# Key products of five tile pairs as seven half products, with the folded query weights parked in device memory

## The chip, the cores and the metric

The kernel runs on one core of one Trainium2 chip. The core's engines are TensorE (PE for its matmuls, PEld for its weight loads), VectorE (DVE), ScalarE (ACT), GpSimd (POOL) and SyncE (SP, which here only issues DMAs). The metric is the time of one execution on the device in microseconds, the median over several runs; lower is better.

## The reference, cut to what matters

Input x is 2048 x 576, with 32 heads of 18. All data is float32.

```python
xn = layernorm(x)                                     # no affine part
q, k, v = split_heads(xn @ wqkv)
phi(t) = concat(softmax(t @ w_phi), softmax(-(t @ w_phi)))   # per head, 36 features
kv  = sum over rows of phi(k)^T v                     # per head 36 x 18
z   = sum over rows of phi(k)
o   = (phi(q) @ kv) / (phi(q) @ z + 1e-6)
s   = o @ wo
g   = silu((silu(xn @ w_gate) * (xn @ w_up)) @ w_down)   # 576 -> 4608 -> 576
return x + s * g
```

## The kernel before, in words

Every float32 operand is held as a high part and a low part, both float32r (`split`: the high part is a cast on ACT, the low part a subtraction on DVE). A product is then the sum of high x high, high x low and low x high, each a matmul of its own. Since 576 is 4.5 blocks of 128 rows, a 576-deep product is 14 matmuls: `xw` issues them, with the last half blocks folded into rows of one plane. `XB` holds the normalized x, transposed, in eight blocks of 512 columns: X00 to X13 in the listings.

The time goes through these stages.

1. Preparation (0 to 66.6 us): layer norm, transposes into `XB`, and `fold`, which multiplies the key and the query weights with w_phi once, so that phi needs one product per tile. The folded key weights and the value weights lie in `KVWH` (high parts, 3 planes of rows) and `KVWL` (low parts, 2 planes), the folded query weights in `QH` and `QL`.
2. Key/value stage (66.6 to 221.6 us): 16 tiles of 128 rows of x in eight pairs p. For each tile: the key product (`k_tile`, 28 matmuls of 288 columns into a bank pair `p2`), the two softmaxes (`softmax_parts`: on DVE max and min over a head and a subtraction for each, exp on ACT, sum on DVE; then reciprocal and multiply), the value product, and `kv_step`, which adds phi^T v into the banks `kvp`. In pairs 0 and 1 the value products are plain. From pair 2 on, the value products of the two tiles of a pair are computed together as seven half products (Strassen's scheme, `v_product`): the needed sums of the value weights are `TH` and `TL` (made by `v_sums` during pair 0, on POOL and ACT), the needed sums of x are `shi` and `slo` (made one pair ahead by `raw_x`, `sums` and `sum_parts`, on POOL and ACT, from `sraw`, one plane of which is loaded from `x_dram`).
3. Query stage (221.6 to about 460 us): 16 query tiles (`q_tile`), two at a time: product with `QH`/`QL` into `p2`, softmaxes as above into `e`, the denominator and the scaling of `e` on DVE (its last step is `last_e`, L626). Then, for each two tiles, transposes and the numerator (`numer`) and the product with wo (`project`).
4. FFN (to the end): gate and up products (L781) and down products (L898).

Between them lie "early tiles": products of the first FFN blocks f = 0 to 3 with `XB` (bank `pe`, L96, 28 matmuls of 512 columns for a tile of gate and up), whose results go to device memory. `early_weights` splits their weights (`raw` into `wh`, `wl`), `early_tile` does the products, Silu on ACT and a multiply with the up product on DVE (`h`, L135).

The order on each engine is fixed at build: a list scheduler places the instructions by its own costs, and `tc.high_priority()` and `tc.issue_after(instruction)` steer it. The holds that matter here refer to two lists: `read` collects the subtractions that read a bank pair (L316, two per `softmax_parts`), `exps` the last exp of each tile. These lines use them:

```python
parts = first_weights.pop() if f == 1 else early_weights(
    f, *{0: read[2 * NT + 1:2 * NT + 2], 2: (read[2 * NT + 3], exps[NT + 1])}.get(f, ()))
for i in halves:
    early_tile(f, i, parts, (1,) if f == 1 else (0, 1), behind=read[2 * NT + 1] if f == 1 else None)
```

NT is 16. `behind` holds the multiply of f = 1; for f = 0 and f = 2 the held instructions are those that split the weights. DMAs are issued in order on SP's queue unless another engine's is named.

## Time and profile before

| | before |
|---|---|
| median of 3 runs | 1594.09 us (1593.2 to 1594.78) |
| profiled execution, its time | 1594.86 us |
| its span on the core | 1592.7 us |
| PE busy | 1580.9 us, 99% |
| DVE busy | 1173.7 us, 74% |
| ACT busy | 724.5 us, 45% |
| POOL busy | 666.0 us, 42% |
| mean granted TensorE clock | 0.999 of full |

A row of the page's parts or of a view has a line of the kernel (L96), an engine, an operation, "out<-in" by the program's names without numbers (`p2` shows as `p`), shapes and counts. In the timeline the first number is the start in us from the beginning of the span, the second the duration, and a bracket at the end gives the idle time before and what released the engine. Matmuls overlap, so the distance between two starts, not the duration, is what one costs.

### The profile page before, as it was taken

Reading aid. Unit: us, or ns where it says so; the run is one execution under the profiler, and the core shown is the slowest. Engines: PE = TensorE matmul, PEld = TensorE weight load, DVE = VectorE, ACT = ScalarE, POOL = GpSimd, SP = SyncE. Lnnn points to the kernel's source line nnn. Section 1 sums busy time; section 2 is a strip of 40 time slices with the busy share of each in tenths; the row PEclk is TensorE's granted clock in tenths of the full one; section 3 lists DMA queues with packets and bytes.
Section 4 is the critical chain, followed back from the end, with each engine's and each line's share of the span. In section 5 each row is a group of like instructions: output and inputs, shape, how many; then the busy total and the mean of one; then the engine's idle time right before and its main releaser. Section 6 shows DMA issues by size and latency. Waiting matters only on the chain.

```text
span 1592.7 us, 25339 instructions
## 1 busy us (share of the span) xinstructions
PE 1580.9 (99%) x9383; PEld 1415.4 (89%) x9383; DVE 1173.7 (74%) x1729; ACT 724.5 (45%) x1403; POOL 666.0 (42%) x714
## 2 busy tenths in 40 slices
PE   9999999999999999999999999999999999999998
PEld 6899998999988988988888888888888888888887
DVE  7777769999946778987777878645667767666577
ACT  5633345455435654444454454454343333333334
POOL 2676762434126545554645535223324324133133
PEclk9999999999999999999999999999999999999999
DMA  9522244445456555555455453964545555565535
GB/s 306 199 82 80 95 148 127 118 124 164 160 181 239 177 180 177 177 173 181 171 183 190 154 188 116 346 212 149 154 142 156 184 180 159 180 183 178 145 117 179
DMA packets 124045, 269.04 MB, mean 169 GB/s; under 512 B 13194, under 2 KB 54858, under 8 KB 122642
## 3 DMA queue, kind: packets, MB, share of 16 engines
q1 hardware_dynamic: 108476, 245.49, 47.0%
q0 software_dynamic: 3552, 12.59, 2.7%
q10 hardware_dynamic: 11894, 9.35, 1.8%
q8 instruction: 74, 1.21, 0.3%
q14 instruction: 49, 0.40, 0.1%
HBM read 167.53 MB, written 99.09 MB: 167 GB/s over the span
## 4 chain that ended last, share of the span: by engine, by line
PE 69%; DVE 1%; POOL 0%; DMA 0%; issue 0%
PE px L781 25%; PE pd L898 24%; PE pw L781 12%; PE py L781 6%; POOL acc L936 0%; PE pe L96 0%; PE pd L781 0%; DMA out<-acc 0%; DVE hh L63 0%; DVE X L927 0%; DVE s L815 0%; DVE ha L831 0%; DVE acc L1098 0%; DVE acc L933 0%; DVE w L63 0%
## 5 line engine op out<-in xcount | busy, mean ns | idle before, releaser
L898 PEld LDWEIGHTS pd<-dw,hh 128*128 128x128 f32 x3012 | 423.8, 188 | 22.1 <-ACT pd L953 1.5
L898 PE MATMUL pd<-dw,hh 128*128 128x288 f32 x3012 | 438.3, 295 | 1.1 <-ACT pd L953 0.7
L781 PE MATMUL px<-X,w 128*128 128x512 f32 x1512 | 386.4, 390 | 0.0
L781 PEld LDWEIGHTS px<-X,w 128*128 128x128 f32 x1512 | 274.5, 188 | 48.9 <-ACT s L810 2.3
L781 PE MATMUL pw<-X,w 128*128 128x512 f32 x744 | 190.4, 391 | 0.0
L781 PEld LDWEIGHTS pw<-X,w 128*128 128x128 f32 x744 | 138.6, 188 | 29.1
L815 DVE TENSOR_TENSOR s<-pw,s 128x512 f32<-128x512 f32 x126 | 86.4, 687 | 97.7 <-ACT s L810 87.7
L1060 DVE TENSOR_TENSOR acc<-pd,acc 128x576 f32<-128x576 f32 x128 | 96.2, 752 | 77.7 <-PE pd L898 77.2
L810 ACT COPY s<-px 128x512 f32<-128x512 f32 x126 | 73.8, 586 | 156.3 <-PE px L781 156.3
L63 DVE TENSOR_TENSOR hh<-ha,hh 128x512 fp32r<-128x512 f32 x140 | 109.4, 807 | 22.2 <-ACT hh L62 21.4
L62 ACT CAST hh<-ha 128x512 fp32r<-128x512 f32 x140 | 82.7, 620 | 87.5 <-PE pd L898 74.2
L1032 POOL TENSOR_TENSOR hb<-hb 128x512 f32<-128x512 f32 x34 | 46.6, 1369 | 160.2 <-DVE hb L827 159.6
L96 PE MATMUL pe<-X,wh 128*128 128x512 f32 x340 | 105.7, 396 | 1.2 <-DVE h L135 0.7
L63 DVE TENSOR_TENSOR w<-ld,w 128x512 fp32r<-128x512 f32 (+1 forms) x96 | 80.5, 840 | 32.5 <-ACT w L62 31.0
L781 PE MATMUL px<-X,wt 128*128 128x512 f32 x252 | 98.0, 389 | 0.0
L1019 POOL TENSOR_TENSOR h<-ha,hb 128x512 f32<-128x512 f32 x34 | 44.4, 1307 | 126.4 <-DVE ha L831 93.9
L781 PE MATMUL py<-X,w 128*128 128x512 f32 x378 | 97.0, 391 | 0.0
L62 ACT CAST w<-ld 128x512 fp32r<-128x512 f32 (+1 forms) x96 | 52.7, 550 | 90.7 <-POOL ld L769 58.3
L1045 POOL TENSOR_TENSOR ha<-ha 128x512 f32<-128x512 f32 x34 | 52.6, 1564 | 94.9 <-DVE hh L63 94.9
L835 ACT COPY py<-px 128x512 f32<-128x512 f32 x63 | 36.0, 572 | 104.4 <-PE px L781 80.0
L766 POOL TENSOR_TENSOR ts<-ld 128x256 f32<-128x256 f32 x32 | 27.4, 855 | 129.9 <-issue 71.5
L781 PEld LDWEIGHTS py<-X,w 128*128 128x128 f32 x378 | 67.8, 188 | 10.6
(293 smaller groups left out, 3229.1 us busy)
## 6 DMA issues: line engine op xcount, KB each, us to landing
w_dram<-w SPq DMA_DIRECT2D x90, 512.0 KB
w<-w_dram SPq DMA_DIRECT2D x90, 512.0 KB
wt<-t_dram SPq DMA_DIRECT2D x62, 336.0 KB
ld<-in_B_w_gu SPq DMA_DIRECT2D x32, 512.0 KB
rt<-in_B_w_down SPq DMA_DIRECT2D x33, 288.0 KB
rb<-in_B_w_down SPq DMA_DIRECT2D x33, 288.0 KB
w_dram<-w SPq DMA_DIRECT2D x30, 256.0 KB
w<-w_dram SPq DMA_DIRECT2D x30, 256.0 KB
```

The costliest lines, as they stand in the source:

```text
L62: nc.scalar.copy(hi, src)
L63: nc.vector.tensor_sub(lo, src, hi)
L96: last = nc.tensor.matmul(ps, l, r, start=n == 0, stop=n == len(pairs) - 1)
L781: nc.tensor.matmul(ps, l, r, start=first and n == 0, stop=last and n == len(mm) - 1, skip_group_check=True)
L810: snaps.append(nc.scalar.copy(t, ps))
L815: nc.vector.tensor_add(t, ps, t)
L835: copies.append(nc.scalar.copy(yp, xp))
L898: nc.tensor.matmul(ps, l, r, start=first and n == 0 and m == 0, stop=n == len(hs) - 1 and m == 2, skip_group_check=True)
L1019: sub(s, g["h"][0][0], g["h"][0][1])
L1032: nc.gpsimd.tensor_add(a21, a21, g["h"][1][1])
L1045: sub(a12, a12, g["h"][0][0])
L1060: nc.vector.tensor_add(a2, pd[:, :, 0:HALF], a2)
```

## The change

For pairs 3 to 7 (`KS = 3`) the key products of the two tiles of a pair are computed as seven half products too, by a new function `pair`, which takes the place of the two `k_tile` calls; the x sums `shi` and `slo` that the value products use serve for the keys as well. The key weights' sums are new. They are made by `k_sums` in pair 1, on DVE, POOL and ACT, plane by plane (c = 0, 1, 2), in two column blocks of 160 and 128 (`wh` and `wl` from the early tiles' pool), with small DMAs on SP for the third plane's rows.

The sums lie where `QH` and `QL` were (tiles of the same names, called `KTH` and `KTL` in the code). So the folded query weights, 2.95 MB, are stored in `q_dram` after the fold and loaded again (`q_weights`, on SP) after the last key product of pair 7. Since the two tiles' key products end in SBUF rows and not in a bank pair, `softmax_rows` does their softmaxes; it appends to `exps`, and not to `read`. The kv steps of a pair and its last value product are carried over into the next pair (`steps`). All else is as before.

```diff
+KS = 3
+    q_dram = dram.tile([P, 2, 5, D], F32, name="q_dram")
...
+            def q_weights():
+                qs = [const.tile([P, 2, n, D], F32R, name=name) for n, name in ((3, "QH"), (2, "QL"))]
+                for t, c in zip(qs, (slice(0, 3), slice(3, 5))):
+                    nc.sync.dma_start(t.bitcast(F32), q_dram[:, :, c])
+                return qs
+
+            def softmax_rows(e):
+                m = kk.tile([P, 2, H], F32, name="m", bufs=1)
+                for s, op in enumerate((ALU.max, ALU.min)):
+                    nc.vector.tensor_reduce(m[:, s], heads(e[:, 0:D]), axis=AX.X, op=op)
+                for s in (1, 0):
+                    nc.vector.tensor_sub(heads(e[:, s * D:(s + 1) * D]), heads(e[:, 0:D]), spread(m[:, s], H))
+                    last = nc.scalar.activation(e[:, s * D:(s + 1) * D], e[:, s * D:(s + 1) * D], AF.Exp,
+                                                scale=1.0 if s == 0 else -1.0)
+                exps.append(last)
...
+            def k_sums():
+                spaces = [(epool.tile([P, 2, 2, 160], F32, name="wh", bufs=3), slice(0, 160)),
+                          (epool.tile([P, 2, 2, 128], F32, name="wl", bufs=3), slice(160, HALF))]
+                kh, kl = k_split(KVWH), k_split(KVWL)
+                nc.vector.memset(KTH[96:128, :, 2].bitcast(F32), 0.0)
+                for c in range(3):
+                    for r, n in spaces:
+                        rows = slice(0, P if c < 2 else 96)
+                        for k in range(2):
+                            if c == 2:
+                                for a in (0, 32):
+                                    nc.sync.dma_start(r[a:a + 32, k], kh[64:96, k, 2, :, n].bitcast(F32))
+                                nc.sync.dma_start(r[64:96, k], kh[0:32, k, 2, :, n].bitcast(F32))
+                            nc.vector.tensor_add(r[rows, k], kh[rows, k, c, :, n], kl[:, k, c, :, n] if c < 2 else r[rows, k])
+                        q = r[rows]
+                        nc.gpsimd.tensor_sub(q[:, 1, 0], q[:, 1, 0], q[:, 0, 0])
+                        nc.gpsimd.tensor_sub(q[:, 0, 0], q[:, 0, 0], q[:, 0, 1])
+                        nc.gpsimd.tensor_add(q[:, 0, 1], q[:, 0, 1], q[:, 1, 0])
+                        nc.gpsimd.tensor_sub(q[:, 1, 1], q[:, 1, 1], q[:, 0, 1])
+                        q = q.rearrange("p k m n -> p (k m) n")
+                        nc.scalar.copy(KTH[rows, :, c, n], q)
+                        if c < 2:
+                            nc.vector.tensor_sub(KTL[:, :, c, n], q, KTH[:, :, c, n])
+                        else:
+                            nc.vector.tensor_sub(KTH[64:96, :, 2, n], q[64:96], KTH[64:96, :, 2, n])
...
+            for n, (t, c) in enumerate(((QH, slice(0, 3)), (QL, slice(3, 5)))):
+                nc.sync.dma_start(q_dram[:, :, c], t.bitcast(F32))
+            KTH = const.tile([P, 4, 3, HALF], F32R, name="QH")
+            KTL = const.tile([P, 4, 2, HALF], F32R, name="QL")
...
+            def pair(n, x, kv0, v3, kv1):
+                v0, v1 = vbuf
+                phi0, phi1 = (kk.tile([P, 2 * D], F32, name="phi", bufs=2) for _ in range(2))
+                pk = kps.tile([P, 2, 512], F32, name="p2")
+                kx, ky = pk[:, 0], pk[:, 1]
+                k_product(kx, x[0], 0, True, False)
+                with tc.high_priority():
+                    nc.scalar.copy(ky[:, 0:HALF], kx[:, 0:HALF])
+                kv0()
+                v3()
+                k_product(ky, x[1], 2, False, True)
+                nc.scalar.copy(phi0[:, K1], ky[:, 0:HALF])
+                kw = kps.tile([P, 512], F32, name="vw")
+                kb = kk.tile([P, HALF], F32, name="kb", bufs=1)
+                k_product(kw, x[7], 1, True, False)
+                with tc.high_priority():
+                    nc.scalar.copy(kb, kw[:, 0:HALF])
+                k_product(kx, x[4], 4, False, False)
+                with tc.high_priority():
+                    nc.scalar.copy(phi0[:, K2], kx[:, 0:HALF])
+                k_product(kw, x[5], 3, False, True)
+                with tc.high_priority():
+                    nc.vector.tensor_add(phi0[:, K2], kw[:, 0:HALF], phi0[:, K2])
+                kv1()
+                k_product(kx, x[6], 5, False, False)
+                with tc.high_priority():
+                    nc.vector.tensor_add(phi1[:, K2], kx[:, 0:HALF], kb)
+                softmax_rows(phi0)
...
+                k_product(kx, x[3], 6, False, True)
+                nc.scalar.copy(phi1[:, K1], kx[:, 0:HALF])
+                q = q_weights() if n == NT - 2 else None
+                softmax_rows(phi1)
...
                         elif j == 0:
                             sums(order[0])
+                            k_sums()
...
+                if p >= KS:
+                    if p == KS:
+                        steps = [lambda: None, lambda: None, lambda: kv_step(*pend)]
+                    raw_x(order[p - 1], 0, 1)
+                    raw_x(order[p - 1], 2, 3)
+                    *steps, q = pair(2 * p, x, *steps)
+                    sums(order[p - 1])
+                    sum_parts(order[p - 1])
+                    load_stack(order[p])
```

The order of the instructions on the engines changes in two places beside the pairs themselves. The first is the beginning of the query stage. On DVE before, the reads of the first query tile (`p2_2479`) are followed at once by the multiply of f = 1 (`h`) and by the splits of f = 0 (`wl`, `wh`):

```order
L315 TENSOR_REDUCE m_2509<-p2_2479 128x32 [waits PE_49]
L316 TENSOR_TENSOR e_2508<-p2_2479,m_2509 128x576 [waits DVE_49]
L315 TENSOR_REDUCE m_2509<-p2_2479 128x32
L316 TENSOR_TENSOR e_2508<-p2_2479,m_2509 128x576 [waits DVE_49]
L135 TENSOR_TENSOR h_4777<-pe_4762,h_4777 128x512 [waits DMASW2_49,PE_49,Activation_49]
L67 TENSOR_TENSOR wl_4797<-raw_4795,wh_4796 128x512 [waits DMAHW1_49]
L67 TENSOR_TENSOR wl_4804<-raw_4802,wh_4803 128x512 [waits DMAHW3_49,Activation_49]
L68 TENSOR_TENSOR wh_4803<-raw_4802,wh_4803 32x2x128
L68 TENSOR_TENSOR wh_4796<-raw_4795,wh_4796 32x2x128
L323 TENSOR_REDUCE sm_2516<-e_2508 128x64 [waits Activation_49]
```

In the changed kernel that multiply and those splits (now L137 and L68) stand on DVE some 180 instructions later, behind the reads of the 11th query tile (`p2_3807`):

```order
L317 TENSOR_REDUCE m_3837<-p2_3807 128x32 [waits PE_49]
L758 TENSOR_TENSOR e_3623<-e_3623,y_3635 128x1152 [waits DVE_49]
L318 TENSOR_TENSOR e_3836<-p2_3807,m_3837 128x576 [waits DVE_49]
L317 TENSOR_REDUCE m_3837<-p2_3807 128x32
L64 TENSOR_TENSOR pl_3725<-pt_3719,ph_3724 72x512 [waits Activation_49]
L64 TENSOR_TENSOR pl_3745<-pt_3739,ph_3744 126x512 [waits Activation_49]
L318 TENSOR_TENSOR e_3836<-p2_3807,m_3837 128x576 [waits DVE_49]
L137 TENSOR_TENSOR h_4854<-pe_4839,h_4854 128x512
L68 TENSOR_TENSOR wl_4874<-raw_4872,wh_4873 128x512
L68 TENSOR_TENSOR wl_4881<-raw_4879,wh_4880 128x512
```

What moved is f = 1's multiply and f = 0's splits, from the 1st to the 11th query tile. On PE before, the second query tile's product (`p2_2529`) is followed by the early products of f = 0:

```order
L96 MATMUL p2_2529<-QL_95,X11_65 128x288
L96 MATMUL p2_2529<-QH_94,X11_65 128x288 x2
L96 MATMUL pe_4809<-X00_60,wl_4797 128x512
L96 MATMUL pe_4809<-X00_60,wh_4796 128x512 x2
L96 MATMUL pe_4809<-X00_60,wl_4797 128x512
```

In the changed kernel the next query tile (`p2_2755`) and the transposes of the first one (`pt`) follow the second tile's product (`p2_2606`):

```order
L98 MATMUL p2_2606<-QL_2337,X11_65 128x288
L98 MATMUL p2_2606<-QH_2336,X11_65 128x288 x2
L98 MATMUL p2_2755<-QH_2336,X10_64 128x288
L98 MATMUL p2_2755<-QL_2337,X10_64 128x288
L98 MATMUL p2_2755<-QH_2336,X10_64 128x288 x2
L98 MATMUL p2_2755<-QL_2337,X10_64 128x288
L98 MATMUL p2_2755<-QH_2336,X10_64 128x288 x2
L770 MATMUL pt_2667<-ident_90,e_2585 72x128
```

After this no `pe` product follows on PE for nine query tiles; when the transposes of the last `e` begin, 249 `pe` products are still to come, where before it were 90.

The second place is the first two pairs of the key stage. On SP in the changed kernel the stores of the query weights stand ahead of the loads for `v_sums` (`sraw`, `slo`, `raw`), and the small DMAs of `k_sums` behind the load from `x_dram`:

```order
L467 DMA q_dram_75<-QL_96 256x1x1152 [waits DMAHW1_49,DVE_49]
L467 DMA q_dram_75<-QH_95 256x1x1728 [waits DMAHW2_49,DVE_49,Activation_49]
L406 DMA sraw_877<-in_A_w_v 128x576 [waits DMAHW5_49,DMAHW6_49,DMAHW3_49,PE_49]
L406 DMA sraw_877<-in_A_w_v 128x576
L406 DMA slo_889<-in_A_w_v 128x576 [waits DMAHW7_49]
L406 DMA raw_888<-in_A_w_v 128x576 [waits DMAHW0_49]
L406 DMA sraw_900<-in_A_w_v 128x576 [waits DMAHW5_49,DMAHW6_49,DMAHW1_49,Pool_49]
L406 DMA sraw_900<-in_A_w_v 128x576 [waits DMAHW2_49]
L115 DMA raw_4872<-in_B_w_gu 128x768 [waits DMAHW3_49,DMAHW0_49,Pool_49]
L365 DMA sraw_999<-x_dram_70 128x4x128 [waits DMAHW2_49,DMAHW4_49,DMAHW1_49,Pool_49]
L433 DMA wh_1095<-KVWH_102 32x2x160 [waits DVE_49]
```

Before, the first of these loads follows directly on the last `wst` load. On ACT before, the exps of the third key tile (`phi_1029`) are followed by the copies of a value bank (`vw_1068`):

```order
L319 ACTIVATE phi_1029<-phi_1029 128x576 [waits DVE_49]
L431 COPY v0_787<-vw_1068 128x90 [waits PE_49,Activation_49]
L431 COPY v0_787<-vw_1068 128x126 [waits Activation_49]
L431 COPY v0_787<-vw_1068 128x72 [waits Activation_49]
L399 CAST KVWH_101<-raw_793 128x2x288 [waits PE_49]
```

In the changed kernel a cast of `k_sums`' third plane, which waits for POOL, stands ahead of those copies, and another ahead of the casts into `KVWH` and `shi`:

```order
L442 CAST QH_798<-wh_1095 96x4x160 [waits DMAHW2_49,DMAHW5_49,DMAHW1_49,DMAHW6_49,DMAHW0_49,DMAHW7_49,DVE_49,Pool_49]
L491 COPY v0_788<-vw_1073 128x90 [waits PE_49,Activation_49]
L491 COPY v0_788<-vw_1073 128x126 [waits Activation_49]
L491 COPY v0_788<-vw_1073 128x72 [waits Activation_49]
L67 CAST wh_4873<-raw_4872 128x768 [waits DMAHW3_49,DVE_49]
L442 CAST QH_798<-wl_1096 96x4x128 [waits DMAHW4_49,DMAHW5_49,DMAHW3_49,DMAHW6_49,DMAHW0_49,DMAHW7_49,DVE_49,Pool_49]
L450 CAST KVWH_102<-raw_794 128x2x288 [waits PE_49]
```

On POOL the eight operations of that plane stand behind `sums` of the first x block. On DVE an addition of the same plane (L435) stands between the second reduction and the second subtraction of the third key tile (`p2_1005`), where nothing stood before:

```order
L317 TENSOR_REDUCE m_1035<-p2_1005 128x32 [waits PE_49]
L318 TENSOR_TENSOR phi_1034<-p2_1005,m_1035 128x576 [waits DVE_49]
L317 TENSOR_REDUCE m_1035<-p2_1005 128x32
L435 TENSOR_TENSOR wh_1095<-KVWH_102,wh_1095 96x320 [waits DMAHW7_49,DMAHW6_49,DMAHW5_49]
L318 TENSOR_TENSOR phi_1034<-p2_1005,m_1035 128x576 [waits DVE_49]
```

So DVE's second subtraction of that tile, the last read of its bank, comes after a wait for DMAs.

More of the change, by code (lines that the diff above doesn't have):

```diff
@@ L461, in v_plain, with k_product, rest @@
                 v_copy(v, pv, i)
+            def k_product(*a):
+                v_product(*a, ws=kws)
+            def pair(n, x, kv0, v3, kv1):
[26 more added lines that the diff above has]
+                softmax_rows(phi0)
+                vx, vy, vw = (kps.tile([P, 512], F32, name=name) for name in ("vx", "vy", "vw"))
+                v_product(vx, x[0], 0, True, False)
+                with tc.high_priority():
+                    nc.scalar.copy(vy[:, 0:HALF], vx[:, 0:HALF])
+                v_product(vw, x[7], 1, True, False)
+                with tc.high_priority():
+                    v_copy(v1, vw, 0)
+                k_product(kx, x[3], 6, False, True)
+                nc.scalar.copy(phi1[:, K1], kx[:, 0:HALF])
+                q = q_weights() if n == NT - 2 else None
+                softmax_rows(phi1)
+                v_product(vx, x[4], 4, False, False)
+                with tc.high_priority():
+                    v_copy(v0, vx, 0)
+                v_product(vw, x[5], 3, False, True)
+                v_add(v0, vw)
+                v_product(vx, x[6], 5, False, False)
+                v_add(v1, vx)
+                v_product(vy, x[1], 2, False, True)
+                v_copy(v0, vy, 1)
+                def rest():
+                    v_product(vx, x[3], 6, False, True)
+                    v_copy(v1, vx, 1)
+                return (lambda: kv_step(n, phi0, v0)), rest, (lambda: kv_step(n + 1, phi1, v1)), q
```

24 lines of the change are left out of this document (19 added, 5 removed).

## The prediction, made before the changed kernel was run

> **What bounds the kernel now.** I read the page first: busy shares and the chain of work that ended last.
>
> ```profile
> PE 1580.9 (99%) x9383; PEld 1415.4 (89%) x9383; DVE 1173.7 (74%) x1729; ACT 724.5 (45%) x1403; POOL 666.0 (42%) x714
> PE 69%; DVE 1%; POOL 0%; DMA 0%; issue 0%
> ```
>
> TensorE is busy for 1580.9 of 1592.7 us, so a matmul saved is worth its time, and a wait put in front of TensorE costs its whole length. The table by windows says which engine stands right behind TensorE in the two stages that the change touches.
>
> ```profile
> core 0: us, PE busy (x) PEld busy (x) DVE busy (x) ACT busy (x) POOL busy (x), PEclk, DMA share, GB/s
> 120.50:138.40 17.90, 17.90 (x147) 17.90 (x146) 13.49 (x18) 6.30 (x18) 11.90 (x12) 1.00 0.26 89
> 66.60:102.60 36.00, 36.00 (x285) 36.00 (x286) 25.20 (x32) 16.03 (x38) 31.95 (x32) 1.00 0.22 66
> 225.60:439.50 213.90, 213.70 (x1436) 197.26 (x1436) 200.25 (x312) 105.11 (x175) 69.83 (x133) 1.00 0.47 144
> ```
>
> A pair in the middle of the key stage (first row) takes 17.90 us and only PE is full. In the first two pairs, 66.6 to 102.6, POOL has 4.05 us free of 36. In the query stage (last row) VectorE works 200.25 of 213.9 us: nearly as full as PE, and PE is full only because early FFN products stand between the query tiles.
>
> **The matmuls saved.** Two key tiles take 2x28 products of 288 columns, seven half products take 7x7=49. That is 7 fewer per pair, 35 over pairs 3 to 7. The first row starts 28 products of one key tile, the second is what follows them.
>
> ```profile
> 102.56 0.29 PE L96 MATMUL p<-KVWH,X 128*128 128x288 f32 x1
> 106.28 0.30 PE L420 MATMUL vx<-KVWH,X 128*128 128x288 f32 x1
> ...
> 107.46 0.38 ACT L500 COPY vy<-vx 128x288 f32<-128x288 f32 x1 [4.13 <-PE vx L420]
> 62.50 0.46 DVE L67 TENSOR_TENSOR QL<-tp,QH 128x288 fp32r<-128x288 f32 x1 [0.82 <-ACT QH L66]
> ```
>
> (106.28-102.56)/28 = 0.133 us each, so 35x0.133 = **-4.6 us**. Each pair gains five copies out of the banks (ACT, 5x0.38=1.9 us by the third row) and two adds of 288 columns (DVE, 2x0.46=0.9 by the fourth). They lie in the 11.6 and 4.4 us that ACT and DVE have free in a pair (row 120.50); the row of a copy behind its product today, 0.38 us, bounds what one late copy could cost PE if that cover were gone: up to 0.4 us a pair, 1.9 in all. I take 0, since nothing in the queue order puts a product right behind the copy that it needs.
>
> **Preparation.** The scheduler puts 7 early products, four DVE adds and eight POOL ops ahead of normalization work in the first 66 us; I take +0.5, between 0 and 2 (7 products of the 0.228 us found below are 1.6).
>
> **Entry of the key stage.** The two stores of the query weights stand on SP ahead of the loads that v_sums reads, and wait for the last fold writes on DVE.
>
> ```profile
> 59.73 0.83 SPq L384 DMA_DIRECT2D sraw<-in_A_w_v  x2
> 62.97 0.30 DVE L68 TENSOR_TENSOR QH<-tp,QH 32x144 fp32r<-32x144 f32 x1
> 45.00:50.00 5.00, 3.93 (x21) 2.88 (x20) 4.49 (x15) 4.65 (x8) 2.06 (x6) 1.00 1.03 372
> 70.14 0.80 POOL L386 TENSOR_TENSOR raw<-sraw 128x288 f32<-128x288 f32 x1
> 83.93 1.92 POOL L385 TENSOR_TENSOR sraw<-sraw 128x288 f32<-128x288 f32 x1
> 89.95 2.81 POOL L348 TENSOR_TENSOR sraw<-X 128x256 f32<-128x256 f32 x4
> 97.39 1.02 POOL L355 TENSOR_TENSOR sraw<-sraw 128x384 f32<-128x384 f32 x1
> 89.73 0.76 DVE L316 TENSOR_TENSOR phi<-p,m 128x576 f32<-128x576 f32 x1
> 93.07 0.29 PE L96 MATMUL p<-KVWH,X 128*128 128x288 f32 x1
> 98.63 2.22 PE L332 MATMUL kvp<-v,phi 128*126 128x127 f32 x20
> 93.32 0.52 ACT L431 COPY v<-vw 128x90 f32<-128x90 f32 x3 [2.11 <-PE vw L96]
> 107.21 0.29 PE L420 MATMUL vw<-KVWH,shi 128*128 128x288 f32 x1
> ```
>
> The stores can start at 63.3 (62.97+0.30). They are 2.95 MB; at the 372 GB/s of a window with the DMA full that is 7.9 us, then come the loads, 1.18 MB or 3.2 us, and about 1 us to issue: 75.5 instead of at most 70.1. POOL starts 5.4 us late. It then has k_sums: four subtractions or additions for each of two column blocks and three planes, 24 ops. From 0.70 (256 wide), 0.80 (288) and 1.02 us (384) I scale 160 columns to 0.47 and 128 to 0.39: 3.4 us a plane. Two planes stand ahead of `sums`, one behind it. `sums` ended at 97.39+1.02=98.4; now 98.4+5.4+6.9-4.05 (POOL's slack) = 106.7, and the third plane's wide block follows at 108.6.
>
> ACT's cast L442 waits for that block, and behind it on ACT stand the value copies for the kv_step that PE began at 98.63: three small copies (0.52, row 93.32) later it can begin at 109.2, **10.6 us** late. Part of this is met earlier: VectorE's L435 of the third plane waits for small DMAs that SP issues behind the x_dram load, which waits for POOL; the second read of that key tile (before at 89.73) stands behind it and slips to about 101, so the product that needs its bank, before at 93.07, slips some 9 us. The two waits are in series on PE, so the later sets the sum. The next consumer, products on `shi` and `slo` (before at 107.21, now 117.8), needs casts and POOL ops that would end near 116.6: nothing more. I take **+11**, between 3 (POOL absorbs its ops, only some of the late loads is left) and 16 (a third of the POOL ops take 1.92 instead of 0.80 us, as the row at 83.93 did).
>
> [...]
>
> **The query stage: who fills PE.** `softmax_rows` appends to `exps` but not to `read`. Before, 16 key tiles left 32 entries, so `read[33]` was the second read of the first query tile. Now only six key tiles append, 12 entries, and `read[33]` belongs to the 11th query tile. The early product f=1's multiply and the weight splits of f=0 and f=2 are held behind it. PE therefore runs out of early products after one of f=0: for nine more tiles it has only query, numerator and projection work, all of it fed by VectorE.
>
> ```profile
> 221.63 0.38 PE L96 MATMUL p<-QH,X 128*128 128x288 f32 x1
> 225.62 0.76 DVE L315 TENSOR_REDUCE m<-p 128x32 f32<-128x576 f32 x1 [0.34 <-PE p L96]
> 225.42 0.39 PE L96 MATMUL pe<-X,wh 128*128 128x512 f32 x1
> 232.02 0.29 PE L96 MATMUL p<-QH,X 128*128 128x288 f32 x1
> 232.05 0.69 DVE L135 TENSOR_TENSOR h<-pe,h 128x512 f32<-128x512 f32 x1 [3.42 <-PE pe L96]
> 438.24 1.36 DVE L626 TENSOR_TENSOR e<-e,y 128x1152 f32<-128x1152 f32 x1
> 438.00 1.28 ACT L131 ACT_TABLE_LOAD   x1 [0.39 <-ACT so L678]
> 439.99 0.82 PE L638 MATMUL pt<-ident,e 128*72 128x128 f32 x6
> L135 DVE TENSOR_TENSOR h<-pe,h 128x512 f32<-128x512 f32 x10 | 6.8, 684 | 3.8 <-PE pe L96 3.8
> ```
>
> An early matmul takes (232.02-225.42)/29 = 0.228 us. By the order of PE, 90 of them were still to come when the last query tile's transposes began (439.99); now 249 are. So 159 x 0.227 = 36.0 us of PE work move behind that point. PE had 439.99-221.63 = 218.4 us to there, all busy; 182.4 us of work are left. VectorE's work shrinks only by the four h multiplies (4x0.684) and some splits, to about 196 us; it starts 4.0 us after PE (225.62) and then waits some 4.7 us for the Silu, a table load (1.28) and the exponentials, an estimate with the 3.42 us below it that VectorE waited there before, for the h multiply. So the last transposes cannot come earlier than 4.0+196+4.7 = 205 us after the stage begins (VectorE without a gap), and at the 94% of before (200.25 of 213.9) they come at 217. PE's idle time is 205-182 = 22 to 217-182 = 35 us. I take **+27**, a little under the middle: with the fillers gone VectorE gets its inputs early, but the chain of a tile (reduce, subtract, exp, sum, multiply) still has gaps. The moved products are no gift later, for PE is full there already. Were the hold harmless, because VectorE's queue lets something else fill PE, it would be 0.
>
> **Reloading the query weights.**
>
> ```profile
> 210.84 0.39 PE L96 MATMUL vy<-X,wh 128*128 128x512 f32 x1
> 217.21 2.22 PE L332 MATMUL kvp<-v,phi 128*126 128x127 f32 x20
> 219.28 1.13 PE L544 MATMUL vx<-ident,zc 126*128 126x126 f32 x8
> PE pe L96 <- DVE h L135: 0.7, 1, 0.7
> ```
>
> The loads go out after the last key product; PE then still has five value products (35x0.133=4.7 us), two kv steps of 2.1 (217.21 to 219.28), the spare early tile (210.84 to 217.21, 6.4) and the zc rows (219.28 to 221.63, 2.3): 17.6 us. The load needs 7.9 us at 372 GB/s and some 2 to begin. Hidden: 0; without that cover up to 3. The one wait of an early product for an h multiply (0.7 us, last row) goes if more products stand behind the query stage: 0 to -0.5, and I take 0.
>
> **Sum.** -4.6+0.5+11+27 = +33.9 on the profiled execution's 1594.86 = 1628.8. That execution is 0.8 above the median of 1594.09, so the median is predicted at **1628**. No change that a measurement can tell is 0.2%, 3.2 us.
>
> **Rivals.**
> 1. *Only the product count matters*: POOL and the DMAs hide the sums, and the hold does not starve PE. For it: PE waits only 11.8 us in the whole run (1592.7-1580.9), so the list order usually fits. Against: VectorE's 200.25 of 213.9 us. 1594.1-4.6 = 1589.5, faster. It decides if both the entry term and the query term are below 4.6 together. 0.05; a balance near zero 0.02.
> 2. *The query stage stays filled* (VectorE runs gapless and PE's queue holds enough work): 1594.1-4.6+0.5+11 = 1601. Against it is that even gapless VectorE needs 205 us. 0.11.
> 3. *The entry is hidden*, the query stage is not: 1594.1-4.1+27 = 1617. POOL's slack would have to be wider than the windows show. 0.10.
> 4. *The clock falls in the new gaps.* Rows: the granted clock was 1.00 in the window 45 to 50, where PE was busy for 3.93 of 5 us, so short gaps cost nothing here; longer ones do not occur. If PE ran at half clock for as long after its gaps as they last, 38 us, it loses half of that: 1628+19 = 1647. 0.08. [...]
>
> My forecast (both terms, clock 1.00) has 0.64. The range 1604 to 1648 leaves out rivals 1 and 2 (0.18); the forecast's own is 1613 to 1641. Slower by over 0.2%: 0.93, faster 0.05, within 0.02.
>
> **What would show it.** Right: the pairs 3 to 7 last about 17.0 us; in the windows of the query stage PE is busy some 85 to 90% and VectorE 95% or more; the first h multiply stands with the 11th query tile; PE's waits name VectorE's e and m lines; VectorE's L435 waits near 90 to 101 and ACT's L442 for POOL to about 109; no query product waits for the DMA of QH; the clock stays at 1.00. Wrong: PE full through the query stage (the +27), or no PE wait from 90 to 110 (the +11), or a lower clock after the gaps (rival 4).

## The result, and the profile after

The changed kernel takes 1657.59 us (median of 4 runs, 1656.3 to 1660.62) against 1594.43 us before: a ratio of 1.0399, with a 95% interval of 1.0386 to 1.0411. It is 63 us slower. 1628 was forecast, with a range of 1604 to 1648: the sign was right, and about half of the size was forecast.

The page of after, busy time and the chain that ended last:

```profile
PE 1596.1 (96%) x9348; PEld 1426.4 (86%) x9348; DVE 1195.3 (72%) x1758; ACT 724.9 (44%) x1424; POOL 687.5 (41%) x738
PEclk9979998999999999999999999999999999999999
PE 83%; DVE 7%; POOL 4%; DMA 3%; ACT 2%; issue 1%; ACTq 0%; SPq 0%; POOLq 0%; DVEq 0%
```

The granted clock of TensorE in the page of before, for comparison:

```profile
PEclk9999999999999999999999999999999999999999
```

The instruction count of PE fell by the 35 products (9383 to 9348), and yet PE is busy for 15.2 us longer (1596.1 against 1580.9). With the 4.65 us that the products should have saved, the remaining matmuls took 19.9 us more. PE is not busy for 62.6 us of the span instead of 11.8. So the span's 66.0 us add up as 50.8 of idle time of PE and 19.9 of slower matmuls, less 4.65; this is bookkeeping for PE alone and does not yet say what caused either. DVE, POOL, DMA and ACT have 7, 4, 3 and 2% of the chain, where before DVE had 1% and the others 0. The row PEclk, all 9 before, has a 7 in the 3rd of its 40 slices and an 8 in the 7th.

The waits of PE in after (us in total, times, longest):

```profile
PE kvp L354 <- DVE phi L507: 15.1, 1, 15.1
PE p L98 <- DVE e L318: 11.0, 3, 6.7
PE pt L770 <- DVE e L758: 8.5, 4, 3.8
PE tp L220 <- DVE xn L208: 3.0, 2, 1.6
PE tp L220 <- POOL xn L211: 2.4, 2, 2.2
PE p L480 <- POOL slo L387: 2.4, 4, 0.9
```

The first is the entry of the key stage, the next two are the query stage, `tp` is preparation, and the last is the pairs. Four places therefore, each named in the prediction, and each came out dearer than its term. The table takes the starts of the first key product, the first query product and the last query transposes in the two traces. The rows of before that the prediction does not show, and those of after; those with `kvp` are the fourth kv step:

```profile
66.56 0.40 PE L96 MATMUL p<-KVWH,X 128*128 128x288 f32 x1
109.99 2.23 PE L332 MATMUL kvp<-v,phi 128*126 128x127 f32 x20
```

```profile
71.07 0.40 PE L98 MATMUL p<-KVWH,X 128*128 128x288 f32 x1 [0.59 <-DVE X L223]
136.89 2.23 PE L354 MATMUL kvp<-v,phi 128*126 128x127 f32 x20
252.05 0.38 PE L98 MATMUL p<-QH,X 128*128 128x288 f32 x1
467.05 0.82 PE L770 MATMUL pt<-ident,e 128*72 128x128 f32 x6
```

| stretch (us) | before | after | difference | forecast |
|---|---|---|---|---|
| to the first key product | 66.56 | 71.07 | +4.5 | +0.5 |
| key/value stage to the first query product | 155.07 | 180.98 | +25.9 | +11 - 4.6 |
| query stage to the last transposes | 218.36 | 215.00 | -3.4 | +27 for this row and the next |
| from there to the end | 1152.7 | 1191.7 | +39.0 | |

The key stage splits at its fourth kv step (109.99 before, 136.89 after): +22.4 to there, +3.5 from there. The last two rows belong together, since the early products that left the query stage stand behind it: +35.6.

### The profile page after: what moved, and what is told of

Its sections match the earlier page's. It is cut to its first block, busy times and chain, and to the rows that moved or that the text cites. A ratio compares the mean times of both kernels' runs of the same rounds, so it can differ in the third digit from the quotient of the medians.

```text
span 1658.7 us, 25359 instructions
## 1 busy us (share of the span) xinstructions
PE 1596.1 (96%) x9348; PEld 1426.4 (86%) x9348; DVE 1195.3 (72%) x1758; ACT 724.9 (44%) x1424; POOL 687.5 (41%) x738
## 4 chain that ended last, share of the span: by engine, by line
PE 83%; DVE 7%; POOL 4%; DMA 3%; ACT 2%; issue 1%; ACTq 0%; SPq 0%; POOLq 0%; DVEq 0%
PE px L913 24%; PE pd L1030 23%; PE pw L913 12%; PE py L913 6%; PE pe L98 5%; PE p L98 3%; PE p L804 3%; PE pt L777 2%; PE kvp L354 1%; PE vw L480 1%; PE pt L770 1%; PE vx L480 1%; DVE m L317 1%; PE p L480 1%; DMA sraw<-in_A_w_v 1%
## 5 line engine op out<-in xcount | busy, mean ns | idle before, releaser
L1030 PEld LDWEIGHTS pd<-dw,hh 128*128 128x128 f32 x3012 | 423.9, 188 | 22.4 <-ACT pd L1085 1.5
L63 ACT CAST w<-ld 128x512 fp32r<-128x512 f32 (+1 forms) x96 | 52.6, 550 | 90.6 <-POOL ld L901 55.8
L1177 POOL TENSOR_TENSOR ha<-ha 128x512 f32<-128x512 f32 x34 | 52.6, 1562 | 95.1 <-DVE hh L64 95.1
L98 PE MATMUL p<-QH,X 128*128 128x288 f32 x320 | 69.3, 312 | 11.0 <-DVE e L318 11.0
```

Source lines behind the costliest of these rows:

```text
L63: nc.scalar.copy(hi, src)
L98: last = nc.tensor.matmul(ps, l, r, start=n == 0, stop=n == len(pairs) - 1)
L1030: nc.tensor.matmul(ps, l, r, start=first and n == 0 and m == 0, stop=n == len(hs) - 1 and m == 2, skip_group_check=True)
L1177: sub(a12, a12, g["h"][0][0])
```

## The experiments

Times are medians in us. Where "against" follows, the second time is the kernel before, measured beside it on the same chip, with their ratio and its interval. Differences between two edited kernels are differences of such medians; the kernel before varied from 1594.28 to 1595.29 between them, so they are good to about 1 us. All kernels named e1 to h2 are the changed kernel with an edit, unless another base is named.

### The hold on `read`

```diff
# e1_read: changed kernel, softmax_rows
-                    nc.vector.tensor_sub(heads(e[:, s * D:(s + 1) * D]), heads(e[:, 0:D]), spread(m[:, s], H))
+                    read.append(nc.vector.tensor_sub(heads(e[:, s * D:(s + 1) * D]), heads(e[:, 0:D]), spread(m[:, s], H)))
# e2_hold: kernel before
-... read[2 * NT + 1:2 * NT + 2], 2: (read[2 * NT + 3], exps[NT + 1]) ... behind=read[2 * NT + 1]
+... read[2 * NT + 21:2 * NT + 22], 2: (read[2 * NT + 23], exps[NT + 1]) ... behind=read[2 * NT + 21]
```

> The changed kernel with softmax_rows appending its two subtractions to read, so that the holds stand at the first query tile again: 90 early products are left at the last transposes, as before. Theory (the shifted hold moves the fillers): the query stage and what follows lose the 35.6 us that the trace shows, 1657.6 - 35.6 = 1622. Rival (the stage is slower because of the reload or the new softmaxes): above 1650.

> The kernel before with the three holds 20 entries later in read, so at the 11th and 12th query tile; nothing else of the change. Theory: 1594.4 + 35.6 = 1630, with gaps of PE on VectorE's e and a granted clock below 1 behind them. Rival (it takes the rest of the change too): 1594 to 1600.

e1_read: 1624.85 (1.0188, interval 1.0173 to 1.0203), 32.7 us less than the changed kernel. e2_hold: 1629.34 against 1595.29 (1.0218, 1.0202 to 1.0233), +34. The index alone, without anything else of the change, costs what the query stage of the changed kernel lost; putting it back takes it away. This is shown from both sides. The windows from the first query product to the last transposes, of e2_hold and of e1_read (columns as in the prediction's table of windows):

```profile
219.80:436.10 216.30, 193.90 (x1309) 182.45 (x1309) 197.41 (x307) 90.39 (x161) 75.72 (x136) 0.94 0.37 109
```

```profile
250.33:469.80 219.47, 218.72 (x1470) 201.73 (x1470) 203.29 (x316) 107.31 (x179) 70.70 (x134) 1.00 0.45 140
```

With the hold late PE is idle for 216.30-193.90 = 22.4 us, and DVE works 197.41 of 216.30. 182.4 us of PE work were forecast for this stretch; it was busy for 193.9, 11.5 more, at a mean granted clock of 0.94. With the hold early, PE is busy for 218.72 of 219.47 at a clock of 1.00.

The stretches of e2_hold's query stage at half clock (columns: length, PE busy, granted clock, DMA share, GB/s):

```profile
237.68:244.51 6.83, 6.36 (x26) 0.50 0.09 25
247.92:254.75 6.83, 3.97 (x17) 0.50 0.16 35
302.53:305.95 3.42, 3.42 (x17) 0.50 0.15 34
326.43:333.25 6.82, 5.28 (x24) 0.50 0.20 55
357.15:360.56 3.41, 3.41 (x17) 0.50 0.25 85
```

PE was busy for 22.4 us in them. How much slower its work is at 0.50 is read from after: products of 288 columns start 0.240 us apart at 0.50 (128.25 to 130.65) and 0.133 at 1.00 (131.39 to 132.72), and the 20 matmuls of a kv step take 3.92 us at 0.50 (110.17 to 114.09) and 1.98 at 1.00 (121.60 to 123.58). By these two, 45 to 49% of the 22.4 us, so an estimated 10.0 to 11.1, is what the lower clock made PE's work longer: most of the 11.5. It does not follow that the stage is 11.5 us longer for it. VectorE works for 197.41 us of it and waits for PE only 2.5 (for ACT 13.4), which speaks for VectorE setting the pace; then PE would have waited in some of the time in which it worked slowly.

### Where the clock fell

The same can be seen at single gaps of after. The entry of the key stage in windows of 5 us (columns: length, PE busy, granted clock, DMA share, GB/s), and two kv steps of 20 matmuls, the first behind the wait and the second 11 us later:

```profile
95.00:100.00 5.00, 0.04 (x1) 0.70 0.00 0
100.00:105.00 5.00, 0.00 (x0) 0.50 0.21 61
105.00:110.00 5.00, 0.00 (x0) 0.50 0.20 52
110.00:115.00 5.00, 4.83 (x27) 0.60 0.11 29
115.00:120.00 5.00, 5.00 (x40) 1.00 0.02 5
```

```profile
110.17 4.17 PE L354 MATMUL kvp<-v,phi 128*126 128x127 f32 x20 [15.13 <-DVE phi L507]
121.60 2.22 PE L354 MATMUL kvp<-v,phi 128*126 128x127 f32 x20
283.18 0.58 PE L98 MATMUL p<-QH,X 128*128 128x288 f32 x1 [6.72 <-DVE e L318]
```

PE stopped at 95.0; the clock was at 0.50 by 100 and still low for some 4 us after work resumed at 110. The kv step took 4.17 us instead of 2.22, so this gap cost PE its own length and about 2 us more. In the query stage the gap of 6.72 us ends in a window (282 to 286) with a granted clock of 0.50. So the clock was at 0.50 behind both gaps, and behind the first it was at 1.00 from 115 on; behind shorter waits it fell in some places and not in others, as the last section shows. No kernel was run that has the gaps at a full clock, so what the clock alone costs is read from windows and not measured by itself.

### The sums made later: two misses

```diff
# e3_late (with the hold still late), e4_both (with the hold early)
-KS = 3
+KS = 4
# k_sums called at the end of pair 2, stores of the query weights at the end of pair 1
+                        with tc.issue_after(exps[-1].ins):
+                            park()
...
+                    with tc.issue_after(exps[-2].ins):
+                        k_sums()
```

> The changed kernel with KS = 4 (four pairs, 28 products saved), the sums of the key weights held behind the exps of pair 2 and the stores of the query weights behind those of pair 1; the hold still shifted (229 early products left at the last transposes). Theory (prep and entry pay for the early sums): prep and entry lose their 4.5 + 22.4 us and the wait of the first pair goes: 1594.4 - 3.7 + 30 to 35 = 1621 to 1626. Rival (the half products or stores themselves stall): above 1640.

> The kernel of late sums (KS = 4) with the holds at the first query tile as well. Theory: only the saved products are left, 1594.4 - 3.7 = 1590.7, up to 1594 if pairs wait a little. Rival (another cost of the change, such as the reload or the pairs' chains, stays): 1597 or more.

e3_late: 1648.79 against 1595.29, where 1621 to 1626 were expected. e4_both: 1618.17 against 1595.29 (1.0147, 1.0132 to 1.0162). The difference between the two is the hold again (30.6). The rest missed by 27. Part of the cause is that these holds bind only instructions of the engine on which the named exp runs, ACT: the additions on DVE and the stores on SP went ahead as before, and the key stage still began at 72.1. So the same was tried with holds that bind, one on DVE and one on SP:

```diff
# f3_late: e4_both with
-                    with tc.issue_after(exps[-2].ins):
+                    with tc.issue_after(read[-1].ins):
                         k_sums()
# and, behind v_sums' loads, loads[-1] being the last of them
+                            with tc.issue_after(loads[-1].ins):
+                                park()
```

> The kernel of e4_both (KS = 4) with holds that bind: all additions of k_sums behind the last read of pair 2 on DVE, and the stores on SP behind the loads for v_sums. Theory: preparation and entry are as before, and what is left is -0.93 us a pair by the products, given back by PE's waits for slo (about 0.9 a pair in the trace): 1595 - 4 to 1595 + 2. Rival (the sums cost as much wherever they stand): 1605 or more.

f3_late: 1617.86 against 1595.01 (1.0145, 1.013 to 1.016): the rival. Preparation and entry are now as before (first key product 65.07, third kv step 97.13), but the key stage is 177.2 us long. ACT in pair 2, and PE's product that waits for it:

```profile
131.54 0.72 ACT L443 CAST QH<-wh 128x640 fp32r<-128x640 f32 x1 [10.17 <-POOL wh L441]
132.17 0.39 ACT L635 COPY vy<-vx 128x288 f32<-128x288 f32 x1
```

```profile
132.62 0.61 PE L485 MATMUL vy<-KVWH,X 128*128 128x288 f32 x1 [7.70 <-ACT vy L635]
```

The cast of the sums stood in ACT's queue ahead of a bank's copy of 0.39 us, and waited 10 us for POOL, whose four ops on that block came behind work on x. PE waited 7.7 us for the copy. The list order put the cast there; on the chip POOL was not yet done with the block.

### What of the entry is what

```diff
# f1_stores: e1_read, stores of the query weights behind the loads for v_sums on SP
+                            with tc.issue_after(loads[-1].ins):
+                                park()
# f2_prep: e1_read, additions of k_sums behind the last DVE work of preparation
+                            with tc.issue_after(ones.ins):
                                 k_sums()
# f4_store: kernel before, with the two stores alone
+            for n, (t, c) in enumerate(((QH, slice(0, 3)), (QL, slice(3, 5)))):
+                nc.sync.dma_start(q_dram[:, :, c], t.bitcast(F32))
```

> The kernel of e1_read with the two stores of the query weights issued on SP behind the loads for v_sums instead of ahead of them. In the changed kernel POOL began v_sums at 79.5 instead of 70.1. Theory (the late loads are a large part of the entry's 22 us): POOL starts about 9 us sooner, 1625 - 6 to 9 = 1616 to 1619. Rival (POOL's own queue with the sums of the key weights sets the entry): 1622 to 1625.

> The kernel of e1_read with the additions of k_sums held on DVE behind the preparation's last DVE work, so that preparation has its old order on PE and DVE again. Theory (the sums of the first plane ahead of the normalization cost the 4.5 us of preparation): the key stage begins at about 66.6 instead of 71, but POOL's eight ops (3.9 us) move into the full entry: 1620 to 1625. Rival (the 4.5 us come from something else): key stage still begins at 71.

> The kernel before with the two stores of the query weights alone, on SP ahead of the loads for v_sums. Theory: the loads are 5 to 9 us late and POOL has 4 us free, so 1596 to 1601. Rival (hidden): no change, 1594 to 1596.

> The kernel of e1_read with both edits, stores behind the loads for v_sums (f1_stores, -6.2) and the sums out of preparation (f2_prep, -10.9). If the two are separate terms: 1624.9 - 17 = 1608. If POOL's queue in the entry sets the time whatever starts it, less than the larger alone is added: 1612 to 1616.

f1_stores 1618.68 and f2_prep 1613.99 (e1_read: 1624.85), the second less than its 1620 to 1625; f4_store 1598.79 against 1595.01 (1.0023, 1.0013 to 1.0032). g2_both, with the edits of the first two together, 1618.72 (before: 1594.28), which missed both expectations. What follows:

- The stores alone cost 3.8 us, and 6.2 in the presence of the sums.
- Preparation's 4.5 us were the first plane's additions and the POOL ops behind them: with them held the key stage began at 65.3, where e1_read has 70.9 and the kernels with the old preparation 64.7 to 66.6. The rest of f2_prep's 10.9 us is in the key stage, 173.2 us where e1_read has 179.4.
- The terms do not add. g2_both has a key stage of 178.4 us, f1_stores 172.7, f2_prep 173.2, and the place of PE's longest wait moves: a bank copy on ACT in f1_stores and g2_both (4.8 and 5.8 us), a multiply on DVE in f2_prep (8.7). The edits changed which queue stood behind POOL; none took POOL out of PE's way.

PE's longest wait in f4_store, f1_stores and f2_prep, in this order (us in total, times, longest):

```profile
PE kvp L333 <- ACT v L435: 2.5, 1, 2.5
```

```profile
PE vy L485 <- ACT vy L638: 4.8, 1, 4.8
```

```profile
PE kvp L354 <- DVE phi L507: 11.9, 2, 8.7
```

The first is a value copy behind the casts that the late loads feed, the second a bank copy behind a cast of the sums, the third the softmax of a key tile.

The wait of 15.1 us in after, followed back through the queues (POOL, ACT, DVE):

```profile
79.46 0.80 POOL L408 TENSOR_TENSOR raw<-sraw 128x288 f32<-128x288 f32 x1 [4.89 <-DMA sraw<-in_A_w_v]
106.00 0.45 POOL L440 TENSOR_TENSOR wl<-wl 128x128 f32<-128x128 f32 x1
106.49 0.62 ACT L442 CAST QH<-wl 128x512 fp32r<-128x512 f32 x1 [4.59 <-POOL wl L440]
107.14 0.82 DVE L444 TENSOR_TENSOR QL<-wl,QH 128x512 fp32r<-128x512 f32 x1 [3.49 <-ACT QH L442]
107.88 2.14 DVE L507 TENSOR_TENSOR phi<-phi,sm 128x1152 f32<-128x1152 f32 x1
```

POOL began v_sums at 79.5, worked to 106.45 without a stop, ACT's cast waited for it, DVE's subtraction for the cast, and behind the subtraction stood the last multiply of the second key tile, which the kv step at 110.17 needed: POOL, ACT, DVE and PE, four in-order queues in a row.

### The sums spread out, and left out

```diff
# g3_phased: KS = 5, stores as in f1_stores; for each plane c
+ additions and POOL ops behind the last read of one key tile (DVE)
+ casts and subtractions behind the last exp and read of the next key tile
# g4_const: KS = 3, stores as in f1_stores, no k_sums
+                    nc.vector.memset(KTH[:, :, c].bitcast(F32), 0.01)
+                    nc.vector.memset(KTL[:, :, c].bitcast(F32), 0.0)
```

> KS = 5 (three pairs, 21 products, -2.8 us), holds at the first query tile, stores behind the v_sums loads, and the sums of the key weights spread over pairs 2 and 3: additions and POOL ops of a plane behind one key tile, its ACT casts and DVE subtractions behind the next, so that no cast stands in ACT's queue before POOL can be done. Theory (the sums cost through waits in the in-order queues of ACT and DVE, not through their busy time): 1595 - 3 to 1595 + 3. Rival (busy time of POOL and DVE): 1605 or more, as in f3_late.

> Leaves out the sums of the key weights: a constant is written where they would stand (about 5 us of DVE in pairs 1 and 2), so the output is not the reference's. KS = 3, holds at the first query tile, stores behind the loads for v_sums, reload as in the change. It prices the pairs, the store and the reload without the sums. If the saved products count in full: 1595.0 - 4.65 = 1590 to 1591. If the wait for slo returns nearly all of it: 1594 to 1597. If the store or reload cost by themselves: above 1598.

g3_phased: 1612.35 against 1594.28 (1.0112, 1.0098 to 1.0126), the rival's side again. A whole tile between POOL's ops and the casts was not enough: PE still waited 6.2 us once for DVE's phi and the key stage took 172.6 us. In the trace of g3_phased that wait is the same chain again:

```profile
154.60 0.62 ACT L452 CAST QH<-wl 96x512 fp32r<-96x512 f32 x1 [7.59 <-POOL wl L444]
155.25 0.68 DVE L456 TENSOR_TENSOR QH<-wl,QH 32x512 fp32r<-32x512 f32 x1 [5.75 <-ACT QH L452]
158.06 4.35 PE L354 MATMUL kvp<-v,phi 128*126 128x127 f32 x20 [6.24 <-DVE phi L521]
```

ACT and DVE were idle for 7.6 and 5.8 us, so this wait is not their busy time; POOL, which they waited for, worked on the x sums in between. Against g4_const below, which has no sums, the sums cost some 14 to 27 us wherever they were put (KS from 3 to 5). That it is the waits throughout and not POOL's busy time, as the theory had it, is not shown, since no placement without waits was found.

g4_const: 1597.99 against 1594.28 (1.0023, 1.0014 to 1.0032). Without the sums nearly all is gone: preparation 65.8, key stage 157.2. So the sums are 27 us of e1_read's 1624.85, with the place of the stores in that. But it is still 3.7 us slower than before, with 35 products fewer, between the 1594 to 1597 expected if the wait for slo returns what the products save and the "above 1598" expected if store or reload cost by themselves. Its key stage is 2.1 us longer than before; another 1.6 us lie behind the first query product (1372.6 us from there to the end, before 1371.1; h1_nochain has the same 1372.6), and no run says whether they are the reload's.

### Why the pairs save nothing

```diff
# h1_nochain: g4_const, sum_parts for pairs 4 to 7
+                if k in order[2:7]:
+                    los[k] = los[order[1]]
+                        his[k, a] = his[order[1], a]
# g1_cast: f2_prep, and h2_cast: g4_const, with
+                    with tc.high_priority():
                         tc.keep_in_program_order(nc.scalar.copy(hi, r[:, j]))
```

> The kernel of g4_const (1598.0, key weights' sums left out) that also leaves out making new x sums for pairs 4 to 7: their products use the sums of pair 3, and the sums written to device memory are those too, so the output is not the reference's. Theory (a pair waits for the chain of x sums, cast on ACT and two POOL ops, behind the last read of the one buffer): pairs 4 to 7 take 17.0 us instead of 17.9, 1598.0 - 3 to 4 = 1594 to 1595. Rival (the softmax chain of the pair or its order sets the period): no change, 1597 to 1598.

> The kernel of f2_prep with the ACT casts of the x sums (shi) at high priority, so that both stand ahead of the exps of the pair. In the trace PE waits 0.25 to 0.9 us a pair for slo, whose chain begins when the last product of the pair before has read shi and slo (one buffer). Theory (that chain gives back the saved products): the wait shrinks, 1614.0 - 1 to 4 = 1610 to 1613. Rival (something else lengthens the pairs): 1614 or more.

> The kernel of g4_const with the casts of the x sums at high priority (the edit of g1_cast, which measured -1.7 there), all x sums made. Theory (chain of the x sums): the chain is shorter by the two exps, about 0.3 us a pair as in g1_cast's periods of 17.6: 1596 to 1597. Rival: no change, 1598.

One kv step of successive pairs, of g4_const and of h1_nochain:

```profile
163.41 2.23 PE L354 MATMUL kvp<-v,phi 128*126 128x127 f32 x20
...
181.19 2.25 PE L354 MATMUL kvp<-v,phi 128*126 128x127 f32 x20
```

```profile
180.15 2.33 PE L354 MATMUL kvp<-v,phi 128*126 128x127 f32 x20
...
197.45 2.22 PE L354 MATMUL kvp<-v,phi 128*126 128x127 f32 x20
```

and PE's waits in g4_const that name the x sums:

```profile
PE p L492 <- POOL slo L387: 2.4, 4, 0.9
PE vw L492 <- POOL slo L387: 1.5, 1, 1.5
```

A pair takes 17.8 us in g4_const and 17.3 in h1_nochain, where 17.9 less 0.93, so 17.0, was forecast. (From kv step to kv step a pair of before takes 18.05, 128.04 to 146.09; the forecast's 17.90 was a window cut a little short, and 17.1 was due.) h1_nochain measured 1595.69 against 1594.89 (1.001, 1.0001 to 1.0019), 2.3 us less than g4_const, with the ratio down from 1.0023. The two intervals overlap slightly, so the size is read from the pairs' periods. They agree with a chain: shi and slo have one buffer, the next pair's can only be made when the last product of a pair has read them, a cast on ACT and two POOL ops come in between, and the changed pair reads them in its third key product, where before the 28 plain products of a key tile gave 3.7 us of cover. h1_nochain alone does not prove it, since it takes away those casts and POOL ops themselves too. h2_cast moves only the casts: its pairs take 17.6 (163.86, 181.51 and 199.13), 0.1 to 0.4 less than in g4_const, about the 0.3 that was expected of the chain. It gained nothing on the whole, 1598.28 against g4_const's 1597.99, a miss: its first changed pair waited 2.1 us for slo instead of 1.5, and the clock fell to 0.50 for 3.4 us there (124.48 to 127.90, with products of 288 columns 0.240 us apart), which it did not in g4_const (1.00 from 109.24 to 145). g1_cast's 1612.26 against the 1613.99 of f2_prep is within what two medians differ.

What remains is open in part. With the chain gone the key stage still takes 155.6 us where 155.07-4.65 = 150.4 was forecast. Of these 5.1 us 3.3 are idle time of PE: 2.4 in two waits for slo in the first changed pair, whose x sums h1_nochain still makes, and 0.9 in one for DVE's phi. In the other 1.9 us PE is busy for longer than forecast, at a clock of 1.00, and no run says why.

## Why the prediction was wrong, step by step

- **Products saved, -4.6.** Failed. The count was right, but its cover was not checked for the step that I costed at 0: the pair's x sums. I looked at the new copies and adds and not at the fact that half products replace plain key products as the cover for the chain of shi and slo. h1_nochain and h2_cast put 0.1 to 0.7 us a pair on this chain, with 2.4 us more in the first changed pair; in place of 4.65 us shorter, the key stage is 2.1 us longer in g4_const, and in after it is 3.5 longer from the fourth kv step on. About 2 us of the term stay unexplained.
- **Preparation, +0.5 (0 to 2).** Mis-sized: +4.5. The four additions and eight POOL ops stand ahead of xn's scaling and copies, and PE waited for those twice, with the clock at half behind them. f2_prep shows it by their hold. Since kernels with the old preparation begin the key stage anywhere from 64.7 to 66.6, the size is known to about 1 us. The rows are the two waits and the window from 54 to 56, whose granted clock is 0.50.

```profile
50.15 0.41 PE L220 MATMUL tp<-ident,xn 128*128 128x128 f32 x2 [1.63 <-DVE xn L208]
52.74 4.27 PE L220 MATMUL tp<-ident,xn 128*128 128x128 f32 x22 [2.18 <-POOL xn L211]
54.00:56.00 2.00, 2.00 (x11) 1.84 (x10) 0.00 (x0) 0.26 (x1) 2.00 (x10) 0.50 0.76 296
```

- **Entry, +11 (3 to 16).** Mis-sized and misplaced: +22.4. The mechanism (a cast of the sums waits for POOL, and what stands behind it waits too; loads late by the stores) is shown by f1_stores, f2_prep and g4_const. But I took the third plane's cast for the stall and missed that the first two planes' casts and subtractions (L442, L444) stood the same way ahead of the second tile's phi, one kv step earlier. The third plane, which was to cost 10.6 us, cost one wait of 2.2 (at 127.87, for the second read of the bank). I had also set POOL's lateness (5.4 us) against a preparation on time; v_sums began 9.3 us late, and the short POOL ops took 0.52 and 0.45 us instead of the scaled 0.47 and 0.39. The slow POOL ops of the upper end, 16, occur in both traces: in before the POOL op of 1.92 us at 83.93 runs beside DVE's multiply of phi by sm (83.73, 1.45 us), and the next two, of 0.80 us (85.93 and 86.81), do not; in after the POOL op at 108.89 took 1.99 us beside the same multiply (107.88, 2.14 us), the op of its shape before it, partly beside that multiply, 1.32 and the one behind it 1.00. What such ops add to the 22.4 is not measured.
- **Query stage, +27.** Mis-sized: +35.6. The mechanism was right and is shown by e1_read and e2_hold (-32.7 and +34). The 27 us meant a stage of 182.4+27 = 209.4 us; e2_hold's took 216.3, near the upper end of the 205 to 217 that was worked out. VectorE worked for 197.4 us, close to the 196 taken, so the part that was too small is its gaps: 18.9 us, where 13.4 were left for them (in after it is busy for 92% of the stage, where 95% or more was to be the sign). PE's idle time, 22.4, stands at the lower end of the forecast 22 to 35 only because its matmuls took 11.5 us longer, at a mean granted clock of 0.94. Whether that clock lengthened the stage or only filled PE's waiting is not shown. In after the stage took 215.0, so 32.6 over 182.4, and the other 3.0 us lie behind the last transposes (39.0 less the 36.0 of moved products).
- **Reload, 0.** Right as far as the waits show: the first query product of after starts at 252.05 without a wait, and no wait of PE names the load of QH. The 1.6 us behind the first query product of g4_const are not assigned.
- **Rival 4, the clock.** It had 0.08, and it occurred, at all four places. Its price was worked out as half of 38 us of idle time, 19, by half clock for as long after a gap as the gap lasted. No run shows that length; what the runs showed is 0.50 for 4 us of work behind the gap of 15.1 us. PE's matmuls took 19.9 us longer, with 50.8 us more idle time. That the two numbers are close is luck. In after's nine stretches at 0.50 PE is busy for 31.8 us, and by the 45 to 49% found above the clock itself accounts for an estimated 14.2 to 15.7 of that; and in g4_const, whose clock stays at 1.00 until the last matmuls are done, they take 3.8 us longer than forecast too (1580.0, where 1580.9-4.65 = 1576.25 was due). The trace of before could not show it between matmuls, where its longest gap is 1.07 us, and does show it behind the last one (PE is done at 1586.6, the clock is 1.00 to 1590 and 0.50 from 1590.5 on); that was a reason to give it even odds wherever my own forecast put gaps of several us, not a small chance. With it the same two terms would have given 1647, still 10 us short.

The sum then is 4.5+22.4+3.5+35.6 = 66.0 on the span, where the prediction had 0.5+11-4.6+27 = 33.9. So no single step failed alone: the entry was 11.4 us too low, the query stage 8.6, the pairs 8.1 and preparation 4.0.

## What to carry to other kernels

A list of instructions that later code indexes by position (`read[2 * NT + 1]`) is part of the schedule: whoever adds a variant of a function must see what it no longer appends, for here this alone was half of the loss. Work that is moved into idle time of several engines and passes from one to the next is to be priced by the queues it blocks, not by its busy time alone; look for each cross-engine wait at what stands directly behind it on the in-order engine. And where a forecast opens gaps of several us on TensorE in a kernel that had none, the slower clock behind them (0.50 here behind the gaps of 15.13 and 6.72 us) belongs into the sum, with the question whether TensorE or another engine paces the stage in which it falls.

## What the runs showed that was not expected

The clock fell to 0.50 not only behind the long waits, but in preparation too (52.6 to 56.0 in after), behind two waits of 1.63 and 2.18 us with 0.41 us of transposes between them; in before, one wait of 1.07 us there left it at 1.00 (46 to 50). In after's first changed pair it fell (0.50 from 155.0 to 158.4) behind waits for slo of 1.30 and 0.94 us, 1.2 us of work apart, and the kv step behind them took 3.27 us:

```profile
156.24 3.27 PE L354 MATMUL kvp<-v,phi 128*126 128x127 f32 x20
```

The same two waits, of 1.46 and 0.94 us in h1_nochain and of 1.47 and 0.95 in g4_const, left it at 1.00 (109.24 to 145 in both). So what a short wait does is not settled by its length in these runs.
